# First normalisation split between VectorE and ScalarE, and the weight transposes spread over the first layer, in a single-core state-space plus dense kernel

## The chip, the cores and the metric

The kernel runs on one core of one Trainium2 chip. The metric is the device time of one execution in microseconds (us). A run's span, from its first to its last profiled instruction, is about 2 us shorter than its device time, so differences of spans and of times can be compared. All runs in this document were at a granted TensorE clock of 0.999 to 1.0.

Engines: PE is the matrix engine (PEld its weight loads), DVE is VectorE, ACT is ScalarE, POOL is GpSimd, SP is SyncE, which issues most DMAs here.

## The reference

```python
def _layernorm(x, axis=-1, eps=1e-5):
    m = jnp.mean(x, axis=axis, keepdims=True)
    v = jnp.var(x, axis=axis, keepdims=True)
    return (x - m) / jnp.sqrt(v + eps)

# x: (1, 2048, 1024) bf16; state P = 1024; hidden F = 3584
xn = _layernorm(x)
# branch A: diagonal complex state space
Lam_bar = exp(dt * Lam);  B_bar = ((Lam_bar - 1) / Lam)[:, None] * (B_re + 1j * B_im)
h[t] = Lam_bar * h[t-1] + B_bar @ xn[t]
yA = 2 * real(h @ (C_re + 1j * C_im).T) + xn * Dskip
# branch B: dense, mish, dense
hid = xn @ w1 + b1;  yB = (hid * tanh(softplus(hid))) @ w2
return x + yA + yB
```

## The kernel before

The 2048 rows are worked in four blocks of 512. Each block has 704 matmuls of 512 columns on PE: 224 for the first dense layer, 128 for the projection with B, 224 for the second dense layer and 128 for the product with C. The last two are the "tail" and share one set of eight PSUM banks. A tile of the first layer is 128 of the 3584 hidden features, 28 tiles to a block; its eviction is VectorE's move of the finished tile from its PSUM bank to SBUF. The four tiles of the head are 128 rows each. Block 0 has more to do: a head (load x, normalise four tiles of 128 rows, transpose them on PE), the transposes of B and C by DMA on the sync queue, the tables of sines and cosines (GpSimd computes phases, ScalarE their sines), and the normalisation of block 1 on VectorE. Weights come through a ring of seven slots, each two tiles of the first layer. The sync queue is in order: a ring load stands behind whatever transposes were written before it.

`keep_busy` is a warm-up: matmuls whose result nobody uses, so that PE's clock is up when the real ones come (in the traces the distance from one to the next falls from 0.107 to 0.056 us on the way).

```python
    def first_sums_v(q, h):
        s = q // 2
        vop(lambda e: e.bn_stats(stats[:, s, h, :], xx[:, 0, q, h * 512:(h + 1) * 512]),
            reads=[b_xx[0][q]], writes=[b_stats[s]])

    def first_var_v(q):
        s = q // 2
        vop(lambda e: e.bn_aggr(mv[:, q, :], stats[:, s, :, :]), reads=[b_stats[s]], writes=[b_mv[q]])
        vop(lambda e: e.tensor_scalar(rc(q, 0), mv[:, q, 1:2], EPS, None, op0=ALU.add),
            reads=[b_mv[q]], writes=[b_rs[q]])

    # ... cut: first_mean_a (sum on ScalarE), first_var_a (squares on ScalarE)

    def first_rsqrt(q):
        scale = 1.0 if q % 2 == 0 else 1.0 / D
        aop(lambda e: e.activation(rc(q, 1), mv[:, q, 1:2], AF.Abs_reciprocal_sqrt, scale=scale, bias=kon[:, 2:3]),
            reads=[b_mv[q], b_kon], writes=[b_rs1[q]])

    def first_apply(q):

        v, y, t = (rc(q, n) for n in range(3))
        if q % 2:
            vop(lambda e: e.tensor_scalar(v, mv[:, q, 1:2], 1.0 / D, EPS, op0=ALU.mult, op1=ALU.add),
                reads=[b_mv[q]], writes=[b_rs[q]])
        vop(lambda e: e.scalar_tensor_tensor(out=t, in0=y, scalar=y, in1=v, op0=ALU.mult, op1=ALU.mult),
            reads=[b_rs[q], b_rs1[q]], writes=[b_rs2[q]])
        vop(lambda e: e.tensor_scalar(t, t, -0.5, 1.5, op0=ALU.mult, op1=ALU.add),
            reads=[b_rs2[q]], writes=[b_rs2[q]])
        vop(lambda e: e.tensor_tensor(y, y, t, op=ALU.mult), reads=[b_rs1[q], b_rs2[q]], writes=[b_rs1[q]])
        vop(lambda e: e.tensor_scalar(xn[:, q, :], xx[:, 0, q, :], mv[:, q, 0:1], y,
                                      op0=ALU.subtract if q % 2 == 0 else ALU.add, op1=ALU.mult),
            reads=[b_xx[0][q], b_mv[q], b_rs1[q]], writes=[b_xn[q]])

    def first_transpose(q):
        bank = 6 + q % 2
        for k in range(NK):
            PE.mm(lambda e, k=k: e.transpose(ps16(bank)[:, k * P:(k + 1) * P], xn[:, q, k * P:(k + 1) * P], ident[:]),
                  reads=[b_xn[q], b_ident], writes=[b_ps[bank]], first=k == 0, last=k == NK - 1)

    def first_copy(q, queue):
        dst = xnT[:, :, q * P:(q + 1) * P]
        srcp = ps16(6 + q % 2).rearrange("p (k t) -> p k t", k=NK)
        if queue is AC:
            aop(lambda e: e.copy(dst, srcp), reads=[b_ps[6 + q % 2]], writes=[b_xnT[q]])
        else:
            vop(lambda e: e.tensor_copy(dst, srcp), reads=[b_ps[6 + q % 2]], writes=[b_xnT[q]])

    # ... cut: normalisation of the later blocks (ln_stats_only, ln_rsqrt, ln_scale, ln_skip)

    def keep_busy(n):
        for i in range(n):
            PE.mm(lambda e: e.matmul(ps[:, 4, 0:P], lhsT=ident[:], rhs=ident[:], start=True, stop=True),
                  reads=[b_ident], writes=[b_ps[4]], first=i == 0, last=i == n - 1)

    keep_busy(34)
    PE.op(lambda e: e.transpose(ps16(5)[:, 0:NST], st[:, :], ident[0:NST, 0:NST]),
          reads=[b_st, b_ident], writes=[b_ps[5]])
    keep_busy(16)
    aop(lambda e: e.activation(rs[:, :, 3], kon[:, 2:3].to_broadcast([P, NQ]), AF.Abs_reciprocal_sqrt, bias=kon[:, 2:3]),
        reads=[b_kon], writes=b_rs)
    for h in range(2):
        first_sums_v(0, h)
    first_var_v(0)
    first_sums_v(2, 0)
    first_mean_a(1)
    first_rsqrt(0)
    first_var_a(1)
    first_rsqrt(1)
    first_apply(0)
    first_transpose(0)
    keep_busy(6)
    first_apply(1)
    first_transpose(1)
    keep_busy(8)
    first_copy(0, VE)
    first_copy(1, VE)
    first_mean_a(3)
    first_var_a(3)
    first_rsqrt(3)
    first_sums_v(2, 1)
    first_var_v(2)
    first_rsqrt(2)
    first_apply(2)
    first_apply(3)
    vop(lambda e: e.tensor_copy(par[:, :], ps16(5)[:, 0:NST]), reads=[b_ps[5]], writes=[b_par])
    NSPLIT = 6

    def first_half(f, half):
        s, fi = f // 2, f % 2
        wt = ring[:, s, :].rearrange("p (k f) -> p k f", k=NK)
        ts = slice(half * 256, half * 256 + 256)
        for k in range(NK):
            PE.mm(lambda e, k=k: e.matmul(ps[:, f, ts], lhsT=wt[:, k, fi * P:(fi + 1) * P], rhs=xnT[:, k, ts],
                                          start=k == 0, stop=k == NK - 1),
                  reads=[b_ring[s]] + b_xnT[2 * half:2 * half + 2], writes=[b_ps[f]],
                  first=half == 0 and k == 0, last=half == 1 and k == NK - 1)

    for f in range(NSPLIT):
        first_half(f, 0)
        if f in (2, 3):
            q = f
            first_transpose(q)
            first_copy(q, AC if q == 2 else VE)

    # ... cut: exp(dt), turns()

    def phases(j):

        xs, b_xs = ph_slot(j)
        pop(lambda e: e.tensor_scalar(px[:], iot[:], cj("thp", j), None, op0=ALU.mult),
            reads=[b_iot, b_cs["thp"]], writes=[b_px])
        pop(lambda e: e.tensor_scalar(py[:], px[:], ROUND_MAGIC, -ROUND_MAGIC, op0=ALU.add, op1=ALU.add),
            reads=[b_px], writes=[b_py])
        pop(lambda e: e.tensor_tensor(xs[:], px[:], py[:], op=ALU.subtract),
            reads=[b_px, b_py], writes=[b_xs])

    turns()
    for j in range(NJ):
        phases(j)
        if j == 1:
            for q in range(NQ):
                load_x(PO, 1, q)          # block 1's x, from GpSimd's queue

    # ... cut

    def first_tile(blk, f):
        s = n_item[0] % NRING
        fi, bank, hs = f % 2, f % 8, f % (2 * GF)
        wt = ring[:, s, :].rearrange("p (k f) -> p k f", k=NK)
        if blk == 0 and f < NSPLIT:
            first_half(f, 1)
        for k in range(0 if blk == 0 and f < NSPLIT else NK):
            PE.mm(lambda e, k=k: e.matmul(ps[:, bank, :], lhsT=wt[:, k, fi * P:(fi + 1) * P], rhs=xnT[:, k, :],
                                          start=k == 0, stop=k == NK - 1),
                  reads=[b_ring[s]] + b_xnT, writes=[b_ps[bank]], first=k == 0, last=k == NK - 1)
        if fi == 1:
            item_done()
        if f % GF == 0 and f >= 2 * GF:
            mish_mul(f // GF - 2)
        vop(lambda e: e.tensor_scalar(hb[:, hs, :], ps[:, bank, :], b1(f), None, op0=ALU.add),
            reads=[b_ps[bank], b_par], writes=[b_hbf[hs]])
        if f % GF == GF - 1:
            mish(f // GF)

    def banks_of(j):
        return 2 * ((j + 2) % 4)

    def project_in(blk):
        for j in range(NJ):
            bank = banks_of(j)
            for ci in range(2):
                for k in range(NK):
                    PE.mm(lambda e, j=j, ci=ci, k=k, bank=bank: e.matmul(
                        ps[:, bank + ci, :], lhsT=BT[:, ci, j, k, :], rhs=xnT[:, k, :], start=k == 0, stop=k == NK - 1),
                        reads=[b_BT[j]] + b_xnT, writes=[b_ps[bank + ci]], first=k == 0, last=k == NK - 1)
            u = ps[:, bank:bank + 2, :]
            for s in range(2):
                vop(lambda e, s=s, u=u, j=j: e.tensor_tensor(
                    mt[:, s, :, :], u, tab[:, s, j, :].unsqueeze(1).to_broadcast([P, 2, TB]), op=ALU.mult),
                    reads=[b_ps[bank], b_ps[bank + 1], b_tab[j]], writes=[b_m[s]])
            vop(lambda e, j=j: e.tensor_tensor(hT[:, 0, j, :], mt[:, 0, 0, :], mt[:, 1, 1, :], op=ALU.add),
                reads=b_m, writes=[b_hT[0][j]])
            vop(lambda e, j=j: e.tensor_tensor(hT[:, 1, j, :], mt[:, 0, 1, :], mt[:, 1, 0, :], op=ALU.subtract),
                reads=b_m, writes=[b_hT[1][j]])
            if j == 4 and blk:
                mish_mul(2)
            if j == 7:
                mish_mul(3 if blk else 2)

    # ... cut: recur (VectorE scans), tail (output matmuls into banks 4 to 7, then 0 to 3)

            if f in (7, 8, 9, 10):
                coefficients(f - 7)
            if f in (9, 11, 12, 14):
                ln_skip(0, (9, 11, 12, 14).index(f))
            if f in (13, 15, 17, 18):
                ln_stats_only(1, (13, 15, 17, 18).index(f))
            if f == 19:
                ln_rsqrt()
            if f in (20, 22, 23, 24):
                ln_scale(1, (20, 22, 23, 24).index(f))
            if f < 16 and f % 2 == 0:
                transpose_B(f // 2)
            if f >= 16:
                transpose_C(f - 16)

        for f in range(NF):
            first_tile(blk, f)
            side(f)
        if blk == 0:
            for i in range(12, 2 * NK):
                transpose_C(i)
        project_in(blk)
```

## Time and profile before

| | |
|---|---|
| time, three runs | 624.34, 624.63, 624.67 us |
| time and span of the profiled run | 625.61 us, 623.6 us |
| first real (256-column) matmul | 10.15 us |
| block 0, from there to the first matmul of block 1 | 154.69 us |
| blocks 1, 2, 3 | 151.95, 151.95, 151.98 us |

The block lengths are differences of times in the chain of waits: 10.15, 164.84, 316.79, 468.74 and 620.72 us. Blocks 1 to 3 run at 151.95 / 704 = 0.216 us a matmul without a gap. PE bounds the kernel; only the head and some 2.7 us of block 0 are open to a change.

Kernel before, the page's busy times (us, share of the span, number of instructions):

```profile
PE 613.7 (98%) x2905; PEld 287.2 (46%) x2961; DVE 465.0 (75%) x695; ACT 247.2 (40%) x162; POOL 49.4 (8%) x47
```

Kernel before, PE in order of time in the head (start us, duration us, engine, line, operation, names, shapes, count, and in brackets the idle time before it and what ended it):

```profile
1.41 3.81 PE L458 MATMUL ps<-ident 128*128 128x128 bf16 x34 [1.41 <-POOL kon L328]
...
7.12 0.62 PE L383 MATMUL ps<-ident,xn 128*128 128x128 bf16 x8 [0.57 <-DVE rs L369]
...
8.66 0.62 PE L383 MATMUL ps<-ident,xn 128*128 128x128 bf16 x8 [0.58 <-DVE xn L376]
...
10.15 2.02 PE L499 MATMUL ps<-xnT,ring 128*128 128x256 bf16 x17 [0.43 <-DVE xnT L392]
```

PE waits here for VectorE's normalisation of tiles 0 and 1 (`xn`), then for VectorE's copies of the transposed tiles (`xnT`).

Kernel before, the chain of waits, first layer of block 0 (start us, duration us, what):

```profile
43.32 5.79 PE ps L641 x26
...
49.17 0.53 SPq L316
...
49.74 2.05 SPq L606
...
51.83 1.50 SPq L606
...
53.43 4.14 DMA ring<-in_B_w_dram
...
57.62 3.63 PE ps L641 x16
```

The chain leaves PE and goes over the sync queue (SPq): a ring load (L316), two B transposes (L606), then the next ring load and its 4.14 us of transfer, for which PE waits. In the list of waits this is one line of PE (us in total, times, longest):

```profile
PE ps L641 <- DMA ring<-in_B_w_dram: 1.1, 2, 0.6
```

Kernel before, VectorE in order of time (three of its lines):

```profile
28.63 0.75 DVE L648 TENSOR_SCALAR hb<-ps,par 128x512 bf16<-128x512 f32 x1 [0.56 <-PE ps L641]
...
35.71 0.69 DVE L432 TENSOR_TENSOR xx<-xx,mt 128x1024 bf16<-128x1024 bf16 x1
...
89.57 2.35 DVE L666 TENSOR_TENSOR mt<-ps,tab 128x1024 bf16<-128x1024 f32 x2
```

The first is the eviction of tile 9, the last place for a long time where VectorE waits for PE. From there to 155.6 us VectorE shows no gap of more than 0.14 us. The last is its last eviction of the projection: it ends at 91.92 us, and PE wants those banks at about 94 us (88.71, the start of the tail, and 24 matmuls of 0.216 us on other banks).

Kernel before, GpSimd in order of time:

```profile
16.62 1.59 POOL L521 TENSOR_SCALAR px<-iot,cs 128x512 f32<-128x512 f32 x1 [13.71 <-DVE cs L452]
...
26.58 2.34 POOL L287 DMA_DIRECT2D xx<-in_A_x_dram  x4
```

The phases start at 16.62 us; after two of the eight groups come the four loads of block 1's x.

### The profile page before, as it was taken

The page shows a single profiled execution, that of the slowest core. Times are in us where ns is not written, and L with a number is a line of the kernel's source. Part 1 is how long each engine was busy: PE and PEld are TensorE (multiplying, and loading weights), DVE is VectorE, ACT ScalarE, POOL GpSimd, SP SyncE. Part 2 cuts the span into 40 slices and gives each one's busy share as a digit, 9 for nine tenths or more (in the row PEclk, how much of TensorE's full clock was granted, in tenths as well). Part 3 has the DMA queues.
Part 4 walks back from the last instruction along what each step waited for, and adds up shares of the span by engine and source line. Part 5 has one row for each costly group of instructions (what it writes and reads, how often), then busy time and mean ns, then how long its engine had stood idle before and what let it go on. Part 6 is the DMA issues. An engine that isn't in the chain of part 4 may idle for free.

```text
span 623.6 us, 7360 instructions
## 1 busy us (share of the span) xinstructions
PE 613.7 (98%) x2905; PEld 287.2 (46%) x2961; DVE 465.0 (75%) x695; ACT 247.2 (40%) x162; POOL 49.4 (8%) x47
## 2 busy tenths in 40 slices
PE   8999999999999999999999999999999999999998
PEld 7643444444444444444444444444444444444443
DVE  6799999999457599998047759999624856999603
ACT  6689995440059950000008992000001999000000
POOL 1899000000100000000010000000000000000000
PEclk9999999999999999999999999999999999999999
DMA  9999996750365300764064530295204542042001
GB/s 269 229 200 256 238 210 181 192 167 1 107 199 167 136 1 6 234 172 130 16 187 144 160 101 1 73 229 154 85 35 135 161 143 68 1 133 104 1 0 68
DMA packets 124188, 79.41 MB, mean 127 GB/s; under 512 B 48890, under 2 KB 106490, under 8 KB 124154
## 3 DMA queue, kind: packets, MB, share of 16 engines
q1 hardware_dynamic: 120656, 71.58, 43.5%
q0 software_dynamic: 960, 3.15, 2.0%
q10 hardware_dynamic: 2538, 4.21, 1.8%
q8 instruction: 24, 0.39, 0.3%
q14 instruction: 10, 0.08, 0.0%
HBM read 63.19 MB, written 4.19 MB: 108 GB/s over the span
## 4 chain that ended last, share of the span: by engine, by line
PE 93%; ACT 2%; DVE 1%; issue 1%; DMA 1%; SPq 1%; ACTq 0%; DVEq 0%
PE ps L715 48%; PE ps L641 25%; PE ps L661 18%; PE ps L499 2%; DMA ring<-in_B_w_dram 1%; SPq L606 1%; ACT act L621 1%; ACT act L620 1%; ACT act L619 1%; DVE hb L648 0%; DVE act L626 0%; PE ps L383 0%; ACTq L294 0%; ACT L620 0%; ACT L465 0%
## 5 line engine op out<-in xcount | busy, mean ns | idle before, releaser
L715 PE MATMUL ps<-ring,act 128*128 128x512 bf16 x880 | 193.2, 379 | 0.8
L641 PE MATMUL ps<-xnT,ring 128*128 128x512 bf16 x832 | 183.2, 379 | 1.9 <-DMA ring<-in_B_w_dram 1.1
L619 ACT ACTIVATE act<-hb 128x3584 bf16<-128x3584 bf16 x16 | 50.9, 3183 | 246.1 <-DVE hb L648 245.9
L715 PEld LDWEIGHTS ps<-ring,act 128*128 128x128 bf16 x896 | 87.7, 98 | 105.7
L641 PEld LDWEIGHTS ps<-xnT,ring 128*128 128x128 bf16 x848 | 82.7, 98 | 101.7 <-DMA ring<-in_B_w_dram 2.5
L648 DVE TENSOR_SCALAR hb<-ps,par 128x512 bf16<-128x512 f32 x112 | 82.8, 747 | 55.6 <-PE ps L641 54.2
L661 PE MATMUL ps<-xnT,BT 128*128 128x512 bf16 x500 | 110.5, 379 | 0.6
L715 PE MATMUL ps<-CT,hT 128*128 128x512 bf16 x500 | 110.5, 379 | 0.6
L666 DVE TENSOR_TENSOR mt<-ps,tab 128x1024 bf16<-128x1024 f32 x64 | 75.3, 1219 | 13.3 <-PE ps L661 11.7
L661 PEld LDWEIGHTS ps<-xnT,BT 128*128 128x128 bf16 x512 | 50.1, 98 | 60.4
L715 PEld LDWEIGHTS ps<-CT,hT 128*128 128x128 bf16 x512 | 50.1, 98 | 60.4
L752 DVE TENSOR_TENSOR xx<-ps,xx 128x1024 bf16<-128x1024 f32 (+1 forms) x17 | 19.5, 1160 | 72.5 <-PE ps L715 72.4
L681 DVE TENSOR_TENSOR_SCAN hT<-cs,qi,hT 128x512 bf16<-128x512 f32 x48 | 58.8, 1267 | 0.0
L621 ACT ACTIVATE act<-act 128x3584 bf16<-128x3584 bf16 x16 | 51.0, 3190 | 0.2
L620 ACT ACTIVATE act<-act 128x3584 bf16<-128x3584 bf16 x16 | 51.0, 3190 | 0.2
L686 DVE TENSOR_TENSOR mt<-hT,tab 128x1024 bf16<-128x1024 bf16 x64 | 41.4, 688 | 1.1
L626 DVE TENSOR_TENSOR act<-act,hb 128x3584 bf16<-128x3584 bf16 x16 | 32.3, 2017 | 1.3 <-ACT act L621 1.3
L287 POOL DMA_DIRECT2D xx<-in_A_x_dram x12 | 6.7, 559 | 255.3 <-DVE xx L752 250.8
L595 ACT ACTIVATE ct<-CT,cs 128x512 f32<-128x512 bf16 x16 | 11.5, 718 | 28.8 <-DVE CT L597 24.5
L621 ACT ACT_TABLE_LOAD x16 | 20.5, 1283 | 0.3
L620 ACT ACT_TABLE_LOAD x16 | 20.5, 1283 | 0.3
L681 DVE TENSOR_TENSOR_SCAN hT<-cs,hT 128x512 bf16<-128x512 f32 x16 | 18.7, 1208 | 0.0
(82 smaller groups left out, 277.8 us busy)
## 6 DMA issues: line engine op xcount, KB each, us to landing
ring<-in_B_w_dram SPq DMA_DIRECT2D x112, 512.0 KB, 3.8
out_dram<-xx ACTq DMA_DIRECT2D x15, 256.0 KB, 2.1
xx<-in_A_x_dram POOLq DMA_DIRECT2D x12, 256.0 KB, 5.3
xx<-in_A_x_dram SPq DMA_DIRECT2D x4, 256.0 KB, 3.0
dsk<-in_A_Dskip_dram SPq DMA_DIRECT2D x1, 256.0 KB, 6.3
out_dram<-xx ACTq DMA_DIRECT2D x2, 128.0 KB, 1.7
xnT<-xn SPq DMA_TRANSPOSE x12, 4.5
BT<-in_A_B_re_dram SPq DMA_TRANSPOSE x8, 5.1
```

The source lines that it names most:

```text
L619: aop(lambda e: e.activation(a, hs, AF.Exp), reads=[b_hb[g % 2]], writes=[b_act[g]])
L620: aop(lambda e: e.activation(a, a, AF.Ln, bias=1.0), reads=[b_act[g]], writes=[b_act[g]])
L621: aop(lambda e: e.activation(a, a, AF.Tanh), reads=[b_act[g]], writes=[b_act[g]])
L626: vop(lambda e: e.tensor_tensor(a, a, hs, op=ALU.mult), reads=[b_act[g], b_hb[g % 2]], writes=[b_act[g]])
L641: PE.mm(lambda e, k=k: e.matmul(ps[:, bank, :], lhsT=wt[:, k, fi * P:(fi + 1) * P], rhs=xnT[:, k, :], start=k == 0, stop=k == NK - 1), rea ...
L648: vop(lambda e: e.tensor_scalar(hb[:, hs, :], ps[:, bank, :], b1(f), None, op0=ALU.add), reads=[b_ps[bank], b_par], writes=[b_hbf[hs]])
L661: PE.mm(lambda e, j=j, ci=ci, k=k, bank=bank: e.matmul(ps[:, bank + ci, :], lhsT=BT[:, ci, j, k, :], rhs=xnT[:, k, :], start=k == 0, stop= ...
L666: vop(lambda e, s=s, u=u, j=j: e.tensor_tensor(mt[:, s, :, :], u, tab[:, s, j, :].unsqueeze(1).to_broadcast([P, 2, TB]), op=ALU.mult), rea ...
L681: vop(lambda e, ci=ci, init=init: e.tensor_tensor_scan(out=hT[:, ci, j, :], data0=cj("r", j).to_broadcast([P, TB]), data1=hT[:, ci, j, :], ...
L686: vop(lambda e, s=s: e.tensor_tensor(mt[:, s, :, :], hT[:, :, j, :], tab[:, s, j, :].unsqueeze(1).to_broadcast([P, 2, TB]), op=ALU.mult), ...
L715: PE.mm(lambda e: e.matmul(ps[:, u, :], lhsT=lhsT, rhs=rhs, start=st_, stop=last), reads=reads, writes=[b_ps[u]], first=st_, last=last)
L752: vop(lambda e: e.tensor_tensor(xr, src, xr, op=ALU.add), reads=b_src + [b_x], writes=[b_x])
```

## The change

Its intent: a shorter head (fewer dependent small operations ahead of the first matmul), and no more weight loads stuck behind transposes in the first layer. Six parts:

1. Tiles 0 and 1 are summed on VectorE, tiles 2 and 3 on ScalarE (before: even on VectorE, odd on ScalarE).
2. A square root on ScalarE and one reciprocal on VectorE replace the reciprocal root with a Newton step of three operations.
3. 76 warm-up matmuls in one piece replace 34 and 16; the parameter transpose moves behind the first real matmuls; tile 1's copy is halved over VectorE and ScalarE, and tile 2's copy goes from ScalarE to VectorE.
4. B transposes come after every third tile of the first layer, C transposes almost all in the projection.
5. The loads of block 1's x go behind four phase groups on GpSimd.
6. The normalisation of block 1 moves to later tiles: its statistics from tiles 13 to 18 to tiles 14 to 20, its scaling from tiles 20 to 24 to tiles 23 to 26. (The last of block 0's own skip additions moves from tile 14 to 13.)

```diff
--- before.py
+++ after.py
... (two hunks cut: a block's transposed input gets two halves as separate buffers; one scratch buffer goes)
@@ -337,15 +337,13 @@
         return rs[:, q, n:n + 1]
 
     def first_sums_v(q, h):
-        s = q // 2
+        s = q % 2
         vop(lambda e: e.bn_stats(stats[:, s, h, :], xx[:, 0, q, h * 512:(h + 1) * 512]),
             reads=[b_xx[0][q]], writes=[b_stats[s]])
 
     def first_var_v(q):
-        s = q // 2
+        s = q % 2
         vop(lambda e: e.bn_aggr(mv[:, q, :], stats[:, s, :, :]), reads=[b_stats[s]], writes=[b_mv[q]])
-        vop(lambda e: e.tensor_scalar(rc(q, 0), mv[:, q, 1:2], EPS, None, op0=ALU.add),
-            reads=[b_mv[q]], writes=[b_rs[q]])
 
     def first_mean_a(q):
         aop(lambda e: e.activation(sq[:], xx[:, 0, q, :], AF.Identity, bias=kon[:, 1:2], accum_out=rc(q, 3)),
@@ -357,39 +355,40 @@
         aop(lambda e: e.activation(sq[:], xx[:, 0, q, :], AF.Square, bias=mv[:, q, 0:1], accum_out=mv[:, q, 1:2]),
             reads=[b_xx[0][q], b_mv[q]], writes=[b_sq, b_mv[q]])
 
-    def first_rsqrt(q):
-        scale = 1.0 if q % 2 == 0 else 1.0 / D
-        aop(lambda e: e.activation(rc(q, 1), mv[:, q, 1:2], AF.Abs_reciprocal_sqrt, scale=scale, bias=kon[:, 2:3]),
+    def first_sqrt(q):
+        scale = 1.0 if q < 2 else 1.0 / D
+        aop(lambda e: e.activation(rc(q, 1), mv[:, q, 1:2], AF.Sqrt, scale=scale, bias=kon[:, 2:3]),
             reads=[b_mv[q], b_kon], writes=[b_rs1[q]])
 
     def first_apply(q):
-
-        v, y, t = (rc(q, n) for n in range(3))
-        if q % 2:
-            vop(lambda e: e.tensor_scalar(v, mv[:, q, 1:2], 1.0 / D, EPS, op0=ALU.mult, op1=ALU.add),
-                reads=[b_mv[q]], writes=[b_rs[q]])
-        vop(lambda e: e.scalar_tensor_tensor(out=t, in0=y, scalar=y, in1=v, op0=ALU.mult, op1=ALU.mult),
-            reads=[b_rs[q], b_rs1[q]], writes=[b_rs2[q]])
-        vop(lambda e: e.tensor_scalar(t, t, -0.5, 1.5, op0=ALU.mult, op1=ALU.add),
-            reads=[b_rs2[q]], writes=[b_rs2[q]])
-        vop(lambda e: e.tensor_tensor(y, y, t, op=ALU.mult), reads=[b_rs1[q], b_rs2[q]], writes=[b_rs1[q]])
+        y = rc(q, 1)
+        vop(lambda e: e.reciprocal(y, y), reads=[b_rs1[q]], writes=[b_rs1[q]])
         vop(lambda e: e.tensor_scalar(xn[:, q, :], xx[:, 0, q, :], mv[:, q, 0:1], y,
-                                      op0=ALU.subtract if q % 2 == 0 else ALU.add, op1=ALU.mult),
+                                      op0=ALU.subtract if q < 2 else ALU.add, op1=ALU.mult),
             reads=[b_xx[0][q], b_mv[q], b_rs1[q]], writes=[b_xn[q]])
 
+    ... (cut: tile 1's second half of transposes goes to bank 5, and first_copy takes a range of k)
@@ -458,37 +457,31 @@
             PE.mm(lambda e: e.matmul(ps[:, 4, 0:P], lhsT=ident[:], rhs=ident[:], start=True, stop=True),
                   reads=[b_ident], writes=[b_ps[4]], first=i == 0, last=i == n - 1)
 
-    keep_busy(34)
-    PE.op(lambda e: e.transpose(ps16(5)[:, 0:NST], st[:, :], ident[0:NST, 0:NST]),
-          reads=[b_st, b_ident], writes=[b_ps[5]])
-    keep_busy(16)
-    aop(lambda e: e.activation(rs[:, :, 3], kon[:, 2:3].to_broadcast([P, NQ]), AF.Abs_reciprocal_sqrt, bias=kon[:, 2:3]),
-        reads=[b_kon], writes=b_rs)
-    for h in range(2):
-        first_sums_v(0, h)
-    first_var_v(0)
-    first_sums_v(2, 0)
-    first_mean_a(1)
-    first_rsqrt(0)
-    first_var_a(1)
-    first_rsqrt(1)
+    keep_busy(76)
+    aop(lambda e: e.activation(rs[:, :, 3], kon[:, 2:3].to_broadcast([P, NQ]), AF.Sqrt), reads=[b_kon], writes=b_rs)
+    for q in range(2):
+        first_sums_v(q, 0)
+        first_sums_v(q, 1)
+        first_var_v(q)
+    first_sqrt(0)
+    first_mean_a(2)
+    first_sqrt(1)
+    first_var_a(2)
+    first_sqrt(2)
     first_apply(0)
     first_transpose(0)
-    keep_busy(6)
+    keep_busy(4)
     first_apply(1)
     first_transpose(1)
-    keep_busy(8)
+    keep_busy(4)
     first_copy(0, VE)
-    first_copy(1, VE)
+    first_copy(1, VE, 0, 4)
+    first_copy(1, AC, 4, NK)
     first_mean_a(3)
     first_var_a(3)
-    first_rsqrt(3)
-    first_sums_v(2, 1)
-    first_var_v(2)
-    first_rsqrt(2)
+    first_sqrt(3)
     first_apply(2)
     first_apply(3)
-    vop(lambda e: e.tensor_copy(par[:, :], ps16(5)[:, 0:NST]), reads=[b_ps[5]], writes=[b_par])
     NSPLIT = 6
 
     def first_half(f, half):
@@ -503,10 +496,14 @@
 
     for f in range(NSPLIT):
         first_half(f, 0)
+        if f == 0:
+            PE.op(lambda e: e.transpose(ps16(5)[:, 0:NST], st[:, :], ident[0:NST, 0:NST]),
+                  reads=[b_st, b_ident], writes=[b_ps[5]])
+            vop(lambda e: e.tensor_copy(par[:, :], ps16(5)[:, 0:NST]), reads=[b_ps[5]], writes=[b_par])
         if f in (2, 3):
             q = f
             first_transpose(q)
-            first_copy(q, AC if q == 2 else VE)
+            first_copy(q, VE)
 
     aop(lambda e: e.activation(c("dt"), ldt, AF.Exp), reads=[b_par], writes=[b_cs["dt"]])
     small("a", "dt", lre, ALU.mult)
@@ -572,7 +569,7 @@
     turns()
     for j in range(NJ):
         phases(j)
-        if j == 1:
+        if j == 3:
             for q in range(NQ):
                 load_x(PO, 1, q)
 
@@ -674,6 +671,9 @@
                 mish_mul(2)
             if j == 7:
                 mish_mul(3 if blk else 2)
+            if blk == 0 and j < 7:
+                transpose_C(2 * j + 2)
+                transpose_C(2 * j + 3)
 
     def recur(blk, j):
         for ci in range(2):
@@ -782,25 +782,22 @@
                     table(j)
             if f in (7, 8, 9, 10):
                 coefficients(f - 7)
-            if f in (9, 11, 12, 14):
-                ln_skip(0, (9, 11, 12, 14).index(f))
-            if f in (13, 15, 17, 18):
-                ln_stats_only(1, (13, 15, 17, 18).index(f))
-            if f == 19:
+            if f in (9, 11, 12, 13):
+                ln_skip(0, (9, 11, 12, 13).index(f))
+            if f in (14, 16, 18, 20):
+                ln_stats_only(1, (f - 14) // 2)
+            if f == 22:
                 ln_rsqrt()
-            if f in (20, 22, 23, 24):
-                ln_scale(1, (20, 22, 23, 24).index(f))
-            if f < 16 and f % 2 == 0:
-                transpose_B(f // 2)
-            if f >= 16:
-                transpose_C(f - 16)
+            if f in (23, 24, 25, 26):
+                ln_scale(1, f - 23)
+            if f < 24 and f % 3 == 2:
+                transpose_B(f // 3)
+            if f >= 26:
+                transpose_C(f - 26)
 
         for f in range(NF):
             first_tile(blk, f)
             side(f)
-        if blk == 0:
-            for i in range(12, 2 * NK):
-                transpose_C(i)
         project_in(blk)
         if 0 < blk < NB - 1:
             for q in range(NQ):
```

More of the change, by code (lines that the diff above doesn't have):

```diff
@@ L203, in build_kernel @@
     xnT = sb("xnT", [P, NK, TB], bf16)
-    b_xnT = [Buf("xnT%d" % q) for q in range(NQ)]
+    b_xnT = [Buf("xnT%d" % q, parts=[Buf("xnT%d_%d" % (q, h)) for h in range(2)]) for q in range(NQ)]
     s_xnT = [DmaSem(nc, "d_xnT%d" % q) for q in range(NQ)]
@@ L229, in build_kernel @@
     rs = sb("rs", [P, NQ, 4], f32)
-    b_rs, b_rs1, b_rs2 = ([Buf("rs%s%d" % (n, i)) for i in range(NQ)] for n in "abc")
+    b_rs, b_rs1 = ([Buf("rs%s%d" % (n, i)) for i in range(NQ)] for n in "ab")
     kon = sb("kon", [P, 3], f32)
@@ L376, in first_apply, with bank_T @@
         vop(lambda e: e.tensor_scalar(xn[:, q, :], xx[:, 0, q, :], mv[:, q, 0:1], y,
-                                      op0=ALU.subtract if q % 2 == 0 else ALU.add, op1=ALU.mult),
+                                      op0=ALU.subtract if q < 2 else ALU.add, op1=ALU.mult),
             reads=[b_xx[0][q], b_mv[q], b_rs1[q]], writes=[b_xn[q]])
+    def bank_T(q, k):
+        if q == 1 and k >= NK // 2:
+            return 5
+        return 6 + q % 2
     def first_transpose(q):
-        bank = 6 + q % 2
@@ L382, in first_transpose @@
         for k in range(NK):
-            PE.mm(lambda e, k=k: e.transpose(ps16(bank)[:, k * P:(k + 1) * P], xn[:, q, k * P:(k + 1) * P], ident[:]),
-                  reads=[b_xn[q], b_ident], writes=[b_ps[bank]], first=k == 0, last=k == NK - 1)
-    def first_copy(q, queue):
-        dst = xnT[:, :, q * P:(q + 1) * P]
-        srcp = ps16(6 + q % 2).rearrange("p (k t) -> p k t", k=NK)
+            bank = bank_T(q, k)
+            PE.mm(lambda e, k=k, bank=bank: e.transpose(ps16(bank)[:, k * P:(k + 1) * P],
+                                                        xn[:, q, k * P:(k + 1) * P], ident[:]),
+                  reads=[b_xn[q], b_ident], writes=[b_ps[bank]],
+                  first=k == 0 or bank != bank_T(q, k - 1), last=k == NK - 1 or bank != bank_T(q, k + 1))
@@ L389, in first_copy @@
+    def first_copy(q, queue, k0=0, k1=NK):
+        dst = xnT[:, k0:k1, q * P:(q + 1) * P]
+        bank = bank_T(q, k0)
+        srcp = ps16(bank).rearrange("p (k t) -> p k t", k=NK)[:, k0:k1, :]
+        b_dst = b_xnT[q] if k1 - k0 == NK else b_xnT[q].parts[k0 // 4]
         if queue is AC:
-            aop(lambda e: e.copy(dst, srcp), reads=[b_ps[6 + q % 2]], writes=[b_xnT[q]])
+            aop(lambda e: e.copy(dst, srcp), reads=[b_ps[bank]], writes=[b_dst])
         else:
-            vop(lambda e: e.tensor_copy(dst, srcp), reads=[b_ps[6 + q % 2]], writes=[b_xnT[q]])
+            vop(lambda e: e.tensor_copy(dst, srcp), reads=[b_ps[bank]], writes=[b_dst])
```

## The prediction

> **What bounds the kernel now.** The matrix engine: the busy-share page has PE 98%, DVE 75%, ACT 40%, clock 1.00. In the chain of waits, blocks 1 to 3 take 151.95, 151.95 and 151.98 us for 704 matmuls of 512 columns: 0.216 us apiece, no gap. Nothing there changes. What can be won is the head before the first real matmul (10.15 us, timeline) and block 0: 154.69 us (10.15 to 164.84). Of its extra 2.74 us, about 0.9 are 16 transposes, 0.1 tiles split in halves, and 1.7 waits for weight loads at 49 to 58 us (list of waits: ring DMA). The chain shows why: a weight load issued at 49.17, two B transposes holding the sync queue (2.05 + 1.50 us), then a 4.14 us load.
>
> **What the change does.**
> 1. Head. VectorE sums tiles 0 and 1 in a row (two of 0.71 us each, aggregate 0.21), ScalarE tiles 2 and 3. Newton (0.22+0.15+0.16 us) becomes one reciprocal, about 0.2 us. One table load (1.28 us) either way. Tile 0 is normalised at about 7.4 us instead of 7.07, tile 1 at 8.1 instead of 8.61. The 76 warm-up matmuls (0.107 us, 0.056 from 5.7 us on) last to 7.75; tile 0's transposes start there. Tile 1's copy is halved over two engines (0.69 us to about 0.37 and 0.55). First real matmul near 9.8 us: gain 0.35, less 0.1 for the parameter transpose now behind it.
> 2. B transposes go from a pair per two tiles (3.45 us of PE; a pair holds the queue about 3.6 us, plus a weight load) to one per three (5.2 us). The ring stays ahead: the 1.7 us go. C transposes still end by 90 us, needed at 94: no effect.
> 3. Loads of block 1's x move behind four phase groups on GpSimd: issued near 36.4 us instead of 26.58. They took up to 8.9 us (x tile view): the first lands at 42 to 45, VectorE asks for it at 42.8.
>
> **Critical path.** VectorE has no idle time from 28.6 to 155.6 us (timeline), so idle time there is never made up. Its last eviction of the projection ends at 91.92; PE needs those banks at 94.05, about 92.0 after the change. With VectorE 0.3 us earlier, slack is some 0.4 us: a wait of 0 to 2.6 us for x (about 1.5 expected) hands PE roughly 0.65 us back at the start of block 0's tail.
>
> Clashes add about ±1 us: the Trainium skill ("SBUF — State Buffer", Reading the diagram) says VectorE operations with two SBUF inputs and GpSimd operations that read SBUF lock each other out. [...]
>
> **Sum.** 624.63 − 0.25 (head) − 1.7 (ring) + 0.65 (VectorE stall) = **623.3 us**; 8 in 10: **622.2 to 624.6**. Faster by over 2%: 0.005, within 2%: 0.985, slower: 0.01.
>
> **What would show it.** Head: first 256-column matmul at 9.6 to 10.0 us. Ring: no wait on the ring DMA in block 0. Stall: VectorE's statistics wait on the x load near 43 us, and a PE gap waiting on VectorE at the first output matmuls on banks 0 to 3. Blocks 1 to 3: 151.95 us each.
>
> **What would make it wrong.** If x lands by 42 us: 622.5 or a bit less. If VectorE waits 4 us or more, or meets GpSimd more often, the gain is gone. If ScalarE is late with its half copy, the head gains nothing. If B transposes bunch up behind x loads, ring waits stay.

(One sentence on the lock is cut at the mark. It offered as the trace's example line 416, a VectorE operation of four elements that took 1.26 us instead of 0.17. The times are right, but that operation has one SBUF input, not two. Line 432 of the same trace has two: it took 0.98 us at 31.06 us, with GpSimd at work beside it, and 0.69 us at 35.71.)

## The result, and the profile after

| | before | after |
|---|---|---|
| time, median of 6 runs | 624.62 us | 624.38 us |
| lowest, highest | 624.34, 624.68 | 624.35, 625.06 |
| ratio of the times | | 0.9999 (0.9986 to 1.0012) |
| span of the profiled run | 623.6 us | 622.4 us |
| first real matmul in it | 10.15 us | 9.78 us |
| block 0 in it | 154.69 us | 153.80 us |

A ratio compares the runs of the two kernels in the same rounds, with a 95% interval, so it is not quite the ratio of the medians.

The change made no difference that can be measured, though the two profiles differ by 1.2 us. That is the first thing to explain. The profiled run of the kernel before took 625.61 us, 1.0 us more than the median of its other runs; the profiled run of the changed kernel (624.40 us) lies at its median.

Kernel after, the page's busy times:

```profile
PE 616.7 (99%) x2981; PEld 287.9 (46%) x2981; DVE 464.1 (75%) x684; ACT 246.7 (40%) x162; POOL 50.2 (8%) x47
```

Kernel after, PE in order of time in the head:

```profile
1.41 5.65 PE L457 MATMUL ps<-ident 128*128 128x128 bf16 x76 [1.41 <-POOL kon L328]
7.43 0.62 PE L378 MATMUL ps<-ident,xn 128*128 128x128 bf16 x8 [0.36 <-DVE xn L366]
...
9.78 1.03 PE L492 MATMUL ps<-xnT,ring 128*128 128x256 bf16 x8 [0.54 <-ACT xnT L389]
```

Kernel after, the chain of waits (head, then the start of block 0's tail):

```profile
1.72 4.16 DMA xx<-in_A_x_dram
...
5.90 1.25 ACT sq L349 x2
...
7.38 0.19 ACT rs L360
...
9.05 0.59 ACT xnT L389
...
9.78 1.03 PE ps L492 x8
...
87.17 3.47 PE ps L715 x16
...
90.64 2.37 DVE mt L663 x2
...
93.05 70.54 PE ps L715 x326
```

In the head the chain now runs over the load of tile 2 and ScalarE's pass over it (L349), which stands in ScalarE's order ahead of tile 1's square root (L360). No ring load and no sync queue follow: those waits are gone. A new piece stands at 90.64 us: PE, in the tail, waits for VectorE's last eviction of the projection. The list of waits has it as one new line of PE:

```profile
PE ps L715 <- DVE mt L663: 0.3, 1, 0.3
```

From one matmul's start to the next it costs 0.43 us more than the usual 0.216.

Kernel after, VectorE in order of time:

```profile
28.50 0.75 DVE L645 TENSOR_SCALAR hb<-ps,par 128x512 bf16<-128x512 f32 x1 [0.26 <-PE ps L638]
...
35.76 1.64 DVE L431 TENSOR_TENSOR xx<-xx,mt 128x1024 bf16<-128x1024 bf16 x1
...
44.49 1.41 DVE L400 BATCH_NORM_STATS2 stats<-xx 128x6 f32<-128x512 bf16 x2
...
90.64 2.35 DVE L663 TENSOR_TENSOR mt<-ps,tab 128x1024 bf16<-128x1024 f32 x2
```

Kernel after, GpSimd in order of time:

```profile
15.84 1.58 POOL L518 TENSOR_SCALAR px<-iot,cs 128x512 f32<-128x512 f32 x1 [12.93 <-DVE cs L451]
...
35.18 1.67 POOL L522 TENSOR_TENSOR ph_h<-px,py 128x512 f32<-128x512 f32 x1
36.80 2.34 POOL L287 DMA_DIRECT2D xx<-in_A_x_dram  x4
```

The statistics on block 1's x at 44.49 us show no idle time ahead: x, issued at 36.80 us and on, was there (its first quarter landed at 40.95 us). But VectorE is later than before. It starts the stretch 0.13 us earlier (28.50 against 28.63 us) and ends the last eviction 1.07 us later (92.99 against 91.92). The 1.64 us operation at 35.76 shows how: the same operation took 0.69 us before, and GpSimd's subtract ran from 35.18 to 36.85 us.

### The profile page after: what moved, and what is told of

It reads as the page before. It is cut to its first block, busy times and chain, and to the rows that moved or that the text cites. A ratio compares the mean times of both kernels' runs of the same rounds, so it can differ in the third digit from the quotient of the medians.

```text
span 622.4 us, 7441 instructions
## 1 busy us (share of the span) xinstructions
PE 616.7 (99%) x2981; PEld 287.9 (46%) x2981; DVE 464.1 (75%) x684; ACT 246.7 (40%) x162; POOL 50.2 (8%) x47
## 4 chain that ended last, share of the span: by engine, by line
PE 98%; DMA 1%; DVE 1%; ACT 0%; SPq 0%; issue 0%
PE ps L715 49%; PE ps L638 29%; PE ps L658 18%; PE ps L492 2%; DMA xx<-in_A_x_dram 1%; DVE mt L663 0%; PE ps L378 0%; ACT sq L349 0%; SPq L287 0%; DVE xx L752 0%; ACT xnT L389 0%; DVE xn L366 0%; ACT mv L351 0%; ACT rs L360 0%; DVE rs L365 0%
```

## The experiments

Two quantities are worked out from the traces, the same way for all kernels. The first splits each profiled span by the starts of PE's groups of matmuls. (Where a matmul's record is missing, the gap it leaves in a trace is not a wait. The second and third columns together are 0.16 us less than the block lengths above, which come from the chain of waits.)

| kernel | start: first real matmul | first layer and projection | tail of block 0 | blocks 1 to 3 and end | span |
|---|---|---|---|---|---|
| before | 10.15 | 78.56 | 75.97 | 458.95 | 623.63 |
| before_again | 10.61 | 77.17 | 75.97 | 458.96 | 622.71 |
| spacing_only | 10.65 | 77.18 | 75.97 | 458.95 | 622.76 |
| head_only | 10.47 | 79.33 | 75.97 | 458.95 | 624.72 |
| head_spacing | 9.84 | 79.35 | 75.97 | 458.96 | 624.12 |
| nudge | 9.56 | 77.60 | 75.97 | 458.96 | 622.09 |
| x_early | 9.72 | 77.22 | 76.42 | 458.95 | 622.31 |
| after | 9.78 | 77.22 | 76.42 | 458.96 | 622.38 |
| after_again | 9.48 | 77.22 | 76.47 | 458.96 | 622.13 |
| warm_56 | 9.86 | 77.22 | 76.47 | 458.95 | 622.49 |
| scale_late | 10.30 | 77.22 | 75.97 | 458.96 | 622.45 |
| pool_short | 9.93 | 77.22 | 75.97 | 458.96 | 622.08 |
| best | 9.84 | 77.21 | 75.97 | 458.96 | 621.99 |

The second is "stretched time": over all VectorE operations from the eviction of tile 9 (where VectorE last has time to spare) to 72 us, what each took above the shortest of its kind in the same trace, where that is over 0.15 us. Every operation so counted overlaps a GpSimd operation in its trace.

| kernel | stretched time, us | phases' start to tile 9's eviction, us |
|---|---|---|
| before, before_again, spacing_only | 3.59, 3.57, 3.57 | 12.01, 12.01, 12.02 |
| head_only, head_spacing | 5.26, 5.29 | 12.66, 12.66 |
| nudge | 3.74 | 11.84 |
| after, after_again, warm_56, x_early, scale_late, best | 4.68, 4.70, 4.71, 4.64, 4.69, 4.67 | 12.66 in all six |
| pool_short | 0.00 | 12.65 |

The start of the new head follows a rule that all ten traces with it show. It comes 3.90 or 3.91 us after tile 2's x has landed (5.81 to 5.96 us in after, x_early, head_spacing, warm_56 and best), or 2.05 us after tile 0's transposes begin, if that is later (the other five). Those transposes stood behind the warm-up in head_only, scale_late and pool_short, and behind VectorE's normalisation of tile 0 in nudge and after_again.

### before_again: the kernel before, once more

No edit.

> The kernel before, unchanged, profiled once more. Its profiled run took 625.61 us, about 1.0 us over its other runs (624.34 to 624.68), while each run of the changed kernel lies 2.0 us over its span. Theory A (the first profile of before caught an unlucky run): the new runs have spans of 622.3 to 622.8 us, and the new trace has about 0.5 us of ring waits instead of 1.5. Rival B (the ring waits are always 1.5 us, and profiling costs 1 us): the new trace again has 1.5 us of ring waits and a span near 623.6.

Measured: 624.75 us median (624.57 to 625.18), ratio 1.0002 (0.9989 to 1.0014), spans 622.6 to 623.2 us. Of PE's list of waits the ring DMA is gone; the weight loads keep one line of it:

```profile
PEld ps L641 <- DMA ring<-in_B_w_dram: 0.5, 1, 0.5
```

and PE in order of time has

```profile
10.61 1.58 PE L499 MATMUL ps<-xnT,ring 128*128 128x256 bf16 x13 [0.43 <-DVE xnT L392]
```

Theory A holds, though one run's span (623.2 us) lies above its range: the first profile of before was not a usual run. Its ring waits cost 1.4 us of PE (78.56 against 77.17), the repeat's about 0.2. The start is later too, at 10.61 us instead of 10.15, since x landed later: tile 1's at 4.37 us instead of 3.98, tile 2's at 5.90 instead of 5.04. The two errors of reading lie on opposite sides: against the first profile the new head looks worth 0.37 us and the spacing 1.4; against the repeat the head looks worth 0.8 and the spacing nothing.

Of the 39 runs of the kernel before, five took over 625.2 us (625.61, 625.70, 625.87, 626.21, 626.40). Ring waits are the likely cause, but only the first was profiled, so that is shown for one.

### head_only: the new head, the rest as before

```diff
# against the changed kernel
-        if j == 3:
+        if j == 1:                       # loads of block 1's x early
-            if f in (14, 16, 18, 20): ln_stats_only(...)   # and 22, 23 to 26
+            if f in (13, 15, 17, 18): ln_stats_only(...)   # and 19, 20 to 24
-            if f < 24 and f % 3 == 2: transpose_B(f // 3)
-            if f >= 26: transpose_C(f - 26)                # rest in the projection
+            if f < 16 and f % 2 == 0: transpose_B(f // 2)
+            if f >= 16: transpose_C(f - 16)                # rest before the projection
```

> Only the new head; transposes and x loads as before. Theory A (block 0 of the kernel before runs at the pace of the sync queue, so that an earlier start only lengthens the ring waits): first real matmul at 9.8 us as in the changed kernel, ring waits 0.2 us longer than in the repeat of before, time within 0.15 us of before. Rival (the head is worth what its start shows): 0.2 to 0.35 us faster.

Measured: 626.32 us median (625.91 to 627.57), ratio 1.0030 (1.0017 to 1.0042): 1.8 us slower. Neither theory foresaw that. Its list of PE's waits:

```profile
PE ps L638 <- DMA ring<-in_B_w_dram: 0.8, 2, 0.7
PE ps L658 <- DVE hb L645: 0.8, 1, 0.8
```

The first line is the ring wait that theory A expected. The second is new: in the projection PE waits for VectorE to evict tile 21 of the first layer, whose bank it wants. VectorE is late there, and its stretched time is 5.26 us instead of 3.57. The start was no better than 10.47 us, because the warm-up matmuls lasted until 8.6 us (see warm_56).

### spacing_only: the transposes spread, the rest as before

```diff
-            if f < 16 and f % 2 == 0: transpose_B(f // 2)
-            if f >= 16: transpose_C(f - 16)
+            if f < 24 and f % 3 == 2: transpose_B(f // 3)
+            if f >= 26: transpose_C(f - 26)
# and the remaining C transposes two by two in the projection
```

> Only the spacing of the B and C transposes; head, x loads and normalisation of block 1 as before. Theory A (ring waits gone, worth some 0.5 us in a typical run): no ring wait in block 0, 0.4 to 0.7 us faster than before, VectorE's last projection eviction near 91.9 us and no PE gap there. Rival (worth 1.5 us in every run): 1.3 to 1.6 us faster. If it is no faster at all, something else than the sync queue sets the pace of block 0.

Measured: 624.74 us median (624.38 to 625.11), ratio 1.0001 (0.9988 to 1.0013). No ring wait in the trace, and no gain: first layer and projection take 77.18 us, the repeat of before 77.17. Both sizes expected were too large. The trace shows where the repeat's 0.18 us of ring wait (at 56.70 us) goes. Without it PE is held for 0.18 us at 61.92 us, just behind VectorE's eviction of tile 21, which ends at 61.87. From the start of tile 9's eviction to the end of tile 21's VectorE takes 32.7 us in both traces and in the first one of before: in a usual run VectorE, not the sync queue, sets how soon PE gets through here, and the spacing has nothing to save.

### scale_late: the changed kernel, block 1's scaling behind the projection

```diff
-            if f in (23, 24, 25, 26):
-                ln_scale(1, f - 23)
         project_in(blk)
+        if blk == 0:
+            for q in range(NQ):
+                ln_scale(1, q)
```

> The changed kernel with the four scalings of block 1's normalisation (0.54 us each on VectorE) moved from before the projection to after it. Theory (what is left of block 0's loss is PE waiting for VectorE's last projection eviction, which ends at 93.0 us and is wanted at about 92.4): that eviction ends near 90.9, no PE gap at the tail, span 0.4 us shorter than the changed kernel's, about 622.0 us, time about 623.9. Rival (the gap there is harmless or comes back later in block 0): same as the changed kernel, 624.4.

Measured: 624.29 us median (623.89 to 624.46), ratio to before 0.9990 (0.9977 to 1.0004), so not clear of the noise; spans 621.9 to 622.5. The mechanism holds: the last eviction ends at 91.71 us,

```profile
89.36 2.35 DVE L663 TENSOR_TENSOR mt<-ps,tab 128x1024 bf16<-128x1024 f32 x2
```

there is no PE gap at the tail, and the tail takes 75.97 us instead of 76.42. The start, though, was at 10.30 us, where the changed kernel's profile had 9.78. The head is the same program in both. PE in order of time shows why:

```profile
1.41 7.00 PE L457 MATMUL ps<-ident 128*128 128x128 bf16 x76 [1.41 <-POOL kon L328]
8.25 0.61 PE L378 MATMUL ps<-ident,xn 128*128 128x128 bf16 x8
...
10.30 1.03 PE L492 MATMUL ps<-xnT,ring 128*128 128x256 bf16 x8 [0.54 <-ACT xnT L389]
```

The 76 warm-up matmuls took 7.00 us instead of 5.65, and the transposes of tile 0 stood behind them, with no wait for VectorE in brackets. In the trace the distance from matmul to matmul falls from 0.107 to 0.056 us at 6.92 us here and at 4.05 us in the changed kernel's first profile. That is a new theory (C): the start is a draw on when the clock goes up. As the rule above has it, this is the case in three of the eight traces with 76 matmuls.

### after_again and warm_56: how long the warm-up lasts

after_again has no edit; warm_56 is

```diff
-    keep_busy(76)
+    keep_busy(56)
```

> The changed kernel, unchanged, once more, on the chip of the next three runs. Theory C (its start is set by the 76 warm-up matmuls, which last 5.7 to 7.2 us because the moment at which PE goes from 0.107 to 0.056 us per matmul differs from run to run, 4.05 to 7.67 us so far): start anywhere from 9.8 to 10.5 us, spans spread over 622.3 to 623.2, in step with the start. PE gap of about 0.4 us at the start of block 0's tail, no ring wait. Rival (the head has one fixed length): start at 9.8 again and spans within 0.2 us.

> The changed kernel with 56 warm-up matmuls for 76. Theory C: the warm-up now always ends by 7.4 us, the transposes of tile 0 wait for VectorE and not for PE's own warm-up, start at 9.7 to 9.9 us in every run, spans 622.2 to 622.5, 0.2 to 0.4 us below the repeat of the changed kernel in the mean. Rival: no difference, because ScalarE's pass over tile 2, ahead of tile 1's square root, sets the start; or a start later than 10 us, because PE goes cold in the gap.

Measured on one chip: after_again 624.86 us median (624.11 to 625.32), ratio 1.0003 (0.9991 to 1.0016), spans 622.1, 623.3, 622.9, 622.9, 622.8. warm_56 624.38 us median (624.10 to 625.70), ratio 1.0000 (0.9987 to 1.0012), spans 622.5, 622.4, 622.1, 622.2 and 623.7. The clock went up at 5.10 us in after_again's profile. In warm_56's it went up only at 7.26 us, by the trace's clock record, so all 56 warm-up matmuls ran at the slow rate and still ended in time: its start was 9.86 us.

```profile
1.42 6.07 PE L457 MATMUL ps<-ident 128*128 128x128 bf16 x56 [1.42 <-POOL kon L328]
7.41 0.62 PE L378 MATMUL ps<-ident,xn 128*128 128x128 bf16 x8
...
9.86 1.03 PE L492 MATMUL ps<-xnT,ring 128*128 128x256 bf16 x8 [0.54 <-ACT xnT L389]
```

That start was not set by the warm-up but by the rival named before the run, ScalarE's pass over tile 2, which waited for x until 5.96 us. after_again's start, 9.48 us, is the earliest of all and below the range that theory C gave it; tile 2's x had landed at 5.43 us there. So the warm-up is one of two draws on the start. Moving tile 2's pass behind tile 1's square root was not tried.

Four of warm_56's five runs lie within 0.1 us of where theory C has them, four of after_again's five lie 0.4 us or more above those four's mean of 622.3, and the fifth of each lies on the other side. The means of the spans are 622.58 and 622.80. That the warm-up can hold up the start is shown by the traces of head_only and scale_late. What it costs in the mean is not settled by these two alone: the 623.7 us run was not profiled, and the ratios' intervals overlap. The changed kernel's spread (622.1 to 623.3 us over five runs) is about what theory C expected (622.3 to 623.2), but tile 2's x is part of it.

### head_spacing and x_early: what makes the head alone slow

head_spacing is head_only with the new spacing of the transposes; x_early is head_spacing with the new places of block 1's normalisation, so that it differs from the changed kernel only in

```diff
-        if j == 3:
+        if j == 1:
             for q in range(NQ):
                 load_x(PO, 1, q)
```

> New head and new spacing of the transposes; the loads of block 1's x early, its normalisation at the old places. The head alone was 1.8 us slower than before: its trace had ring waits of about 0.9 us and a PE wait of 0.95 us at the projection for VectorE's eviction of tile 21. Theory D (two separate losses, the spacing cures only the first): no ring wait, the PE wait at the projection of 0.5 to 1 us remains, span 623.0 to 623.8, time about 625.3. Rival (both come from the sync queue): span 622.4, as the changed kernel.

> The changed kernel with only the loads of block 1's x back behind two phase groups (issued near 26 us instead of 36.8). Theory D: no ring wait, no PE wait at the projection (the later places of the normalisation cure that), a gap of 0 to 0.8 us at the tail according to how VectorE meets GpSimd: span 622.3 to 622.9, within 0.4 us of the changed kernel. Rival (the late loads are what keeps the transposes fast): ring waits of over 0.5 us are back, span 623 or more.

Measured: head_spacing 626.17 us median (626.10 to 626.58), ratio 1.0027 (1.0014 to 1.0039); x_early 624.35 us (624.17 to 625.14), ratio 1.0001 (0.9987 to 1.0014).

In head_spacing there is no ring wait, and PE's list has one new long line:

```profile
PE ps L658 <- DVE hb L645: 1.6, 1, 1.6
```

The spacing cures the ring wait alone, as theory D says, but the wait for VectorE grows from 0.95 to 1.8 us from start to start (0.5 to 1 was expected), and the time is 0.9 us above what was expected. So the two waits are not two losses: first layer and projection take 79.33 us with the ring waits and 79.35 without. From tile 9's eviction to the end of tile 21's VectorE takes 34.7 us in both, against 32.7 in before. VectorE alone sets the loss, and the ring waits of head_only lie inside it. In x_early that wait is gone, since VectorE no longer does block 1's scaling ahead of tile 21's eviction: the later places of the normalisation save about 1.7 us of span (622.58 against 624.26 in the mean). Of that debt of lateness 0.44 us comes due at the tail.

x_early and after_again do not differ by more than their spread (622.58 and 622.80 us mean span). Within that spread the late loads of x neither help nor harm.

### nudge: GpSimd's phases 0.8 us later

```diff
# against head_spacing: one more operation ahead of the phases
     turns()
+    pop(lambda e: e.tensor_scalar(px[:, 0:168], iot[:, 0:168], cj("thp", 0), None, op0=ALU.mult),
+        reads=[b_iot, b_cs["thp"]], writes=[b_px])
     for j in range(NJ):
         phases(j)
```

> The kernel of head and spacing (624.1 us span, PE waits 1.79 us for VectorE's eviction of tile 21 at the projection) with one more GpSimd operation ahead of the phases, about 0.65 us long, nothing else. Theory E (the new head starts GpSimd's phases 0.65 us earlier against VectorE's evictions, 12.66 instead of 12.01 us ahead of the eviction of tile 9, and this alone makes VectorE meet GpSimd worse: 5.3 us of stretched VectorE operations after 28 us instead of 3.6, the same in every run): stretched time back to about 3.6 us, PE wait at the projection 0.5 us or less, span about 622.5. Rival (the clashes are chance, or the wait comes from the order of the work on VectorE): span stays near 624.

Measured: 624.65 us median (624.21 to 625.09), ratio 0.9995 (0.9981 to 1.0008); mean span 622.56 us against head_spacing's 624.26. Added work on an engine with time to spare made the kernel 1.5 us faster (medians 624.65 and 626.17, on different chips, both against the same before of 624.6).

GpSimd in order of time, head_spacing first and nudge second:

```profile
15.89 1.59 POOL L518 TENSOR_SCALAR px<-iot,cs 128x512 f32<-128x512 f32 x1 [12.98 <-DVE cs L451]
```

```profile
15.62 0.73 POOL L570 TENSOR_SCALAR px<-iot,cs 128x168 f32<-128x168 f32 x1 [12.70 <-DVE cs L451]
16.44 1.56 POOL L518 TENSOR_SCALAR px<-iot,cs 128x512 f32<-128x512 f32 x1
```

and nudge's wait at the projection:

```profile
PE ps L660 <- DVE hb L647: 0.2, 1, 0.2
```

The added operation and the gap behind it moved the phases by 0.82 us (0.65 was meant). The stretched time fell from 5.29 to 3.74 us and the wait from 1.6 to 0.2. Theory E is shown, and with it why the new head alone was slow: it brings the phases forward by 0.65 us against VectorE's evictions. About 0.4 us of that is the chain of small operations that feeds them (parameters, exponential, phase step): the phases start 6.06 us after the first real matmul instead of 6.47. The rest is tile 9's eviction, 0.24 us later after that matmul, about what the parameter transpose adds to the first layer. The stretched time is not chance. It is the same within 0.1 us in every trace with the same order and alignment.

### pool_short: GpSimd idle after 24 us

```diff
# a wrong result on purpose: one operation for three
-        pop(... px = iot * thp);  pop(... py = round(px));  pop(... xs = px - py)
+        pop(lambda e: e.tensor_scalar(xs[:], iot[:], cj("thp", j), 0.001, op0=ALU.mult, op1=ALU.mult),
+            reads=[b_iot, b_cs["thp"]], writes=[b_xs])
-        if j == 3:
+        if j == 7:
             for q in range(NQ):
                 load_x(PO, 1, q)
```

> The changed kernel with GpSimd doing one operation for three in each phase (a wrong result, on purpose), the x loads behind all eight of them, near 29 us. Theory E: without GpSimd work after 29 us VectorE's stretched time there falls from 4.7 us to under 0.6, its last projection eviction ends at 89.5 to 90 us against 92.8 to 93.0, no PE gap at the tail, span 0.4 us shorter at the same start. Rival (VectorE is late for its own work): eviction at 92 us or later and the gap of 0.4 us stays.

Measured: 623.78 us median (623.35 to 624.10, four runs), ratio 0.9980 (0.9962 to 0.9998). GpSimd was done by 23.7 us, earlier than the 29 expected and before tile 9's eviction. The stretched time is 0.00 us, the last eviction ends at 89.71 us, now at PE's pace, and there is no gap at the tail:

```profile
87.35 2.36 DVE L659 TENSOR_TENSOR mt<-ps,tab 128x1024 bf16<-128x1024 f32 x2 [0.30 <-PE ps L654]
```

VectorE is late because it meets GpSimd, not for its own work. (The time is not a measure of what this is worth: 0.3 us of the gain lies outside the span, and the nine runs of before in this job hold three long ones, see best.)

### best: both leftovers taken away

```diff
# scale_late, and
-    keep_busy(76)
+    keep_busy(56)
```

> The changed kernel with both of block 0's leftovers taken away: the scalings of block 1's normalisation behind the projection, and 56 warm-up matmuls for 76. Expected: no PE gap at the tail, start 9.5 to 9.9 us, spans 621.7 to 622.1, time about 623.9, some 0.7 us below before and the changed kernel, faster than both though far inside 2 per cent. If warm-up or the tail gap is not what is left, it stays at 624.3 or more.

Measured: 623.86 us median (623.66 to 623.98), ratio 0.9982 (0.9968 to 0.9995), result correct, spans 621.7 to 622.0. The clock went up early in its profile (4.27 us), and with 56 matmuls PE then stood ready and waited for VectorE. (The 1.26 us of idling did not slow the transposes, 0.62 us as in the other traces; the start, 9.84 us, again followed tile 2's x, which landed at 5.93.)

```profile
1.41 4.64 PE L457 MATMUL ps<-ident 128*128 128x128 bf16 x56 [1.41 <-POOL kon L328]
7.31 0.62 PE L378 MATMUL ps<-ident,xn 128*128 128x128 bf16 x8 [1.26 <-DVE xn L366]
```

It beats the kernel before by 0.8 us (medians of one job; its longest run is below the shortest of before's nine, 624.31) and the changed kernel by 0.5 to 1.0 us (medians 624.38 and 624.86 of two other jobs). Its five runs lie within 0.3 us of each other, the changed kernel's eleven within 1.2 us. The ratio, like those of nudge and pool_short, counts three long runs of before (625.70 to 626.40) in its nine. The mean of best's five runs is 623.83 us, that of before's other six 624.54.

## Why the prediction was right or wrong

**PE bounds the kernel, blocks 1 to 3 do not move: right.** They take 151.95, 151.95 and 151.96 us after the change.

**Ring waits, 1.7 us to be saved: the step that failed.** The waits vanish, as the prediction put it, and in that pair of traces they are worth 1.4 us. But they were not in the time that was to be predicted. The trace was of a run 1.0 us above the kernel's own median, and the term was sized from that run and subtracted from the median. spacing_only shows what the step is worth in usual runs: nothing measurable (ratio 1.0001), because VectorE's eviction of tile 21 holds PE there as soon as the ring does not.

**Head, 0.25 us: a start at 9.8 us, as put; the size was off in both directions.** The first real matmul came at 9.78 us. The old head started at 10.61 and 10.65 us in its two other traces (before_again, spacing_only), not at 10.15, so the traces allow up to 0.8 us. Part of that is when x happened to land, in both heads. Against that, the prediction took the warm-up to last to 7.75 us each time. In two of the traces with 76 matmuls it lasted past 8.4 us and the start slipped to 10.30 and 10.47 us. And it did not see that ScalarE's pass over tile 2 stands ahead of tile 1's square root, which ties the start to tile 2's x. The parameter transpose, put at 0.1 us, costs about 0.23: from the first real matmul to the end of the 256-column ones PE needs 11.77 us instead of 11.54.

**A new VectorE stall at the start of the tail, 0.65 us: right in place, about right in size (0.43 to 0.49 us), wrong in cause.** It was put down to x landing late. VectorE did not wait for x at all. The first quarter landed at 40.95 us, 4.2 us after its issue, and not at 42 to 45, and VectorE asked at 44.49 us instead of 42.8, being late already; x_early changed nothing. For x landing by 42 us the prediction had 622.5 us or a bit less, and that did not come true either. The lateness came from meeting GpSimd. The prediction named this and called it chance of about ±1 us around zero. It is fixed by alignment: about +1.1 us of stretched time in every trace of the changed kernel's order, shown by nudge and removed by pool_short.

**C transposes have no effect: right.** No trace has a wait on them.

**The sum.** The prediction was 623.3 us, the time 624.38, at the upper end of its range. With the usual run of before as the base the terms are: start 9.78 − 10.61 = −0.83, tail +0.45, parameter transpose +0.23, the repeat's ring wait −0.18: −0.33 us of span (622.38 against 622.71), which is the profile's reading of two ordinary runs. But the starts vary. Their mean is 9.89 us over the eight traces with 76 warm-up matmuls and 10.47 over the three of the old head, which makes −0.58 of the −0.83 and about −0.1 us of the sum (an estimate from few traces). The medians differ by −0.24 us at first and by +0.28 us in after_again's job. That the time still fell inside the predicted range owes something to luck: 1.7 us for the ring waits were missing, and the head gave more than the 0.25 us put for it. "The same" is the right word.

## What to carry to other kernels

Before a profile is used to size a gain, set the profiled run's own time beside the other runs: a wait that is only in an unusually long execution is not in the median. Between engines that hold each other up, as VectorE and GpSimd did here, a small shift of one engine's start against another's can be worth more than the work saved, and it repeats in every run; so try a part of a change alone, and expect that parts which save nothing by themselves pay for the side effects of others. A warm-up of fixed count can outlast the wait for the real work when the clock goes up late; a smaller count avoids that, though what it gains in the mean is not settled here. Before an engine's pass over later data is put ahead of a step on the critical path, ask when those data land.

## What the Trainium skill lacked or had wrong

- "TensorE: Matmul & The Clock Gate" (Part 1: The HAM clock gate) says that the transition comes around 4 us into sustained matmuls, varies by ±500 ns from run to run, and depends on a free-running window. The variation agrees in kind and is larger here: in traces with an unbroken warm-up it came between 2.6 us (after, x_early) and 5.8 us (head_only, warm_56) after the first matmul. What the page lacks is the consequence: a fixed count of warm-up matmuls can itself delay the first real work, here to a start at 10.47 us instead of 9.8.
- "SBUF — State Buffer" (Reading the diagram; Who interferes with whom) has the lock between VectorE and GpSimd, and every trace agrees (1.64 us instead of 0.69 beside GpSimd's subtract; 0.00 us of stretched time without GpSimd). It lacks that the total depends on alignment and repeats: 5.3 us or 3.7 us (head_spacing, nudge) for the same VectorE operations, with GpSimd's phases 0.82 us apart. Some of the operations held had one SBUF input (1.26 us instead of 0.17 for a `tensor_scalar` of four elements); the page also names a 2-port mode of VectorE, but no trace shows an operation's mode.
- No page that was read says how long a DMA transpose holds its queue when other loads are in flight: 256 KB B transposes took 1.2 to 8.0 us of the sync queue here, the longest (7.40 us in the first trace of before, 5.09 in its repeat, 8.04 in head_only) while block 1's x was being loaded.
